# A fused attention and expert kernel: the sums made beside batch 1, X's mixed inputs, and the second layer's first blocks

## The chip, the cores and the metric

The kernel runs on 1 core of one Trainium2 chip. The metric is the time of one execution on the device in microseconds (us), lower is better. The five engines of the core run their own instruction lists: TensorE (PE, with its weight loads shown apart as PEld), VectorE (DVE), ScalarE (ACT), GpSimd (POOL) and SyncE (SP, which here issues nearly all DMAs).

## The reference

```python
def reference(**kwargs):
    ...
    attn_out = _attn_ref(**attn_kwargs)          # 2 x 8 heads x 576 x 64, threshold before the softmax
    x = np.ascontiguousarray(attn_out.transpose(0, 2, 1, 3)).reshape(B * S, H * D)   # 1152 x 512
    x = _moe_ref(x=x, **moe_kwargs)
    return _moe2_ref(x=x, **moe2_kwargs)

def _moe_ref(x, w1, w2, w3, w_out):
    h = np.maximum(np.maximum(x @ w1, x @ w2), x @ w3)    # 512 -> 768
    return (h @ w_out).astype(np.float32)                 # 768 -> 512

def _moe2_ref(x, domain_probs, w1, w2):
    p = domain_probs / (domain_probs.sum(-1, keepdims=True) + 1e-09)
    for e in range(4):
        h = np.maximum(x @ w1[e], 0.0)                    # 512 -> 1024
        out += p[:, e:e + 1] * (h @ w2[e])                # 1024 -> 512
    return out
```

## The kernel before

Every product is made in float32 precision from two parts of each operand: a high half (a copy by ACT, called hi) and a low half (operand less high half, called lo, mostly by POOL), and three matmuls per product. The 1152 rows are worked in two groups: group 0 holds 512 rows of batch 0, group 1 the other 640, batch 1 and the 64 left over.

The order in time is: attention of batch 0; then the first layer (`layer_max`) and the four experts (`experts`) of group 0, and beside the experts the attention of batch 1 (`attention_slow`); then group 1's first layer and experts, which save products by Strassen's scheme (`mixed_pair`: seven products in place of eight, on sums and differences of quarter blocks).

**What sets the order.** All matmuls of the layers form one stream (`Stream`), which counts the columns that it has passed through TensorE. Loads, halves and sums of weights are hooks with a column at which they are written into the program (`plan.at(use - lag, fn)`: so many columns ahead of their use). The results of a product are taken out of PSUM 1000, 2000, ... columns after it. `attention_slow` is a generator: at each yield the main program lets the stream go on by `PACE` columns (L1213 to L1217). PE, DVE, ACT and POOL then run in the order written. SP's order is left to the scheduler. So an instruction that waits holds up all that stands behind it on its engine.

**One step of `attention_slow`** has four yields: scores (`qk`, L331) and their maximum; exponential on ACT (`power`, L349); threshold and row sum on DVE (`weigh`, L354); normalization on POOL (`norm`, L362). The weights of the step before are transposed on PE (`turn`, L372) in the second quarter. A job has 9 steps; four jobs make batch 1. The next job's K and Q are prepared beside it (`prep`, L176 on): transposed, halved (KN on ACT L187 and DVE L189), the 64 remaining rows of k transposed into another PSUM buffer (L192), and spread over the partitions by ten DMAs from SP (L203, L205, L206 and L219).

**Sums for group 1.** A pair of weight blocks needs four sums of its quarters (`quarter_sums`, L845). They are made beside batch 1, by POOL, half a pair at a time (`sums_ahead`): a load, the sums 8000 columns later, a store to DRAM 11000 columns later, one such set every `AHEAD` = 14500 columns, 22 sets. `pair_block` then loads them (tile s) with the raw block (wraw), and makes the halves dh, dl, sh, sl with the lags of LAGS_X or LAGS_PAIR.

**X's mixed inputs** (`mixed_x`, L824): eight differences of quarters of X by DVE (`less`, L809), each with a high half by ACT (L814) and a low half by DVE (L817). They are made after batch 1's attention, in front of group 1's first product, one step for each 1024 columns.

**Blocks of w_out** for group 1 (`weights64` with g = 1, names o0_0 to o3_1): loaded 20000, high half 8000 and low half 6500 columns ahead of use (LAGS_KEPT).

Raw weight blocks use a ring of four buffers (`raw`); their high and low halves are tiles a (first matrix) and b (second matrix).

Of the kernel before, what the change touches and what calls it, by code (L numbers as in the profile page):

```python
# [22 lines left out]
def fused_kernel(ctx: ExitStack, tc: tile.TileContext, q, k, v, tau, w1, w2, w3, w_out, probs, m_w1, m_w2, out):  # L23
    nc = tc.nc
# [24 lines left out]
    LAGS_FIRST = (("words", 60000), ("exponent", 50000), ("low3", 49000), ("clamp", 48000), ("merge", 47000), ("sign", 46000), ("keep", 45000), ("hi", 10500), ("lo", 9000))  # L49
    LAGS_KEPT = (("load", 20000), ("hi", 8000), ("lo", 6500))  # L50

    LAGS_A = ((1.05, 1, 1.4, 1.9), (3, 3, 3, 1.9))
# [13 lines left out]
    START = 13000  # L66
    PACE = 2000
    STACKED = 10000
# [107 lines left out]
    def prep(job):  # L176
# [12 lines left out]
        nc.vector.tensor_tensor(out=KN[:, 1, 0:MAIN], in0=tk, in1=f32(KN[:, 0, 0:MAIN]), op=ALU.subtract)  # L189
        yield  # L190
        tr = ptile_at("U", [P, REM + P])
        nc.tensor.transpose(tr[:, 0:REM], flat(kr), ident[0:REM, 0:REM])  # L192
# [533 lines left out]
    def weights64(g, name, use, src, shape):  # L726
        kept["planned"] = kept.get("planned", 0) + 1
        return block(use, shape, "a", NA, None, (LAGS_FIRST if kept["planned"] <= EARLY else LAGS64, LAGS_KEPT)[g], name, g, src if g == 0 else None)

# [94 lines left out]
    def mixed_x():  # L824
        steps = []
        for c in range(KC // 2):
            b11, b12, b21, b22 = (part("x", d, cols) for d in (c, KC // 2 + c) for cols in (left, right))
            steps += [less(b11, b12, b11), *cut("x", 0, c, b11), less(b12, b22, b12), less(b22, b22, b11),
                      *cut("x", 1, c, b22), *cut("x", 2, c, b12), less(b21, b21, b22), *cut("x", 3, c, b21)]
        return steps  # L830

# [9 lines left out]

    def quarter_sums(S, A):

        for out, a, b, op in ((0, A(1, 0), A(1, 1), ALU.add), (1, S(0), A(0, 0), ALU.subtract), (2, A(0, 0), A(1, 0), ALU.subtract), (3, A(0, 1), S(1), ALU.subtract)):
            nc.gpsimd.tensor_tensor(out=S(out), in0=a, in1=b, op=op)  # L845

    def sums_ahead(when, key, half):
        b = {}

        def load():  # L850
            b["raw"] = atile([P, 2, 2, P], F32, "sraw")
            for i in range(2):
                nc.sync.dma_start(out=b["raw"][:, i], in_=half(i))

        def sums():
            b["s"] = atile([P, 4, P], F32, "ssum")
            quarter_sums(lambda x: b["s"][:, x, :], lambda i, j: b["raw"][:, i, j, :])

        def store():
            key, c = b["key"]  # L860
            if ("s", key) not in kept:
                kept["s", key] = dp.tile([P, 4, 2, P], F32, name=f"kept_s{key}")
            nc.sync.dma_start(out=kept["s", key][:, :, c, :], in_=b["s"])

        b["key"] = key
        for fn, lag in ((load, 0), (sums, 8000), (store, 11000)):
            plan.at(when + lag, fn)

    def pair_block(use, src, lags, key=None):
# [3 lines left out]
        def load():  # L873
            b["raw"] = mix_tile([P, KC, 2 * P], F32, "wraw")
            if isinstance(src, tuple):
                nc.sync.dma_start(out=b["raw"][:, :, 0:P], in_=kept[src[0]])
                nc.sync.dma_start(out=b["raw"][:, KC // 2:KC, P:2 * P], in_=kept[src[1]][:, KC // 2:KC, :])
            else:
                nc.sync.dma_start(out=b["raw"], in_=src)
# [4 lines left out]
        def sums():  # L884
            if key is None:
                quarter_sums(lambda x: b["s"][:, x, :, :], raw)

# [73 lines left out]

    LAGS_X = (27000, 26000, 12800, 11800, 10800, 11600, 9500, 6800)
    LAGS_PAIR = (
        (44000, 30000, 27500, 26500, 25500, 26000, 23500, 21000),
        (44000, 29000, 26500, 25500, 24500, 23500, 21000, 18500))
    LAGS_SOON = ((44000, 42000, 40000, 39000, 37000, 38000, 34000, 30000), (44000, 42000, 36000, 34000, 32000, 33000, 28000, 23000))
    AHEAD = 14500

    def max_mixed():
# [31 lines left out]
        for f in range(0, NF, 2):  # L1001
            for w in range(3):
                for c in range(2):
                    sums_ahead(MAX0 + 10000 + AHEAD * k, (f"w{w}_{f}", c), lambda i, w=w, f=f, c=c: kept[f"w{w}_{f + i}"][:, c::2, :])
                    k += 1
                b = pair_block(plan.cols, (f"w{w}_{f}", f"w{w}_{f + 1}"), LAGS_X, f"w{w}_{f}")
                mixed_pair(b, "x", X[1], finish(f, w), (1, 5, 6, 7, 2, 4, 3))
        for f in range(0, NF2 // 2, 2):
            for c in range(2):
                rows = m_w1[0].rearrange("(j c p) f -> c p j f", j=2, p=P)[c]  # L1010
                sums_ahead(MAX0 + 10000 + AHEAD * k, (f"e{f}", c), lambda i, f=f, rows=rows: rows[:, :, (f + i) * P:(f + i + 1) * P])
                k += 1
# [139 lines left out]
    bufs_a = {"K12": 2, "QS": 2, "V": 2, "VR": 2, "em": 3, "am": 6, "ar": 4}  # L1152
    bufs_b = {"K12": 2, "QS": 2, "em": 2, "am": 4, "ar": 2}
    for bf in (bufs_a, bufs_b):
# [67 lines left out]
    while steps or mo["waiting"]:  # L1222
        if steps:
            steps.popleft()(None)
        if mo["waiting"]:
            mo["waiting"].pop(0)()
        goal = stream.now + 1024
        while stream.now < min(goal, END0):
# [43 lines left out]
```

## Time and profile before

| | |
|---|---|
| median of 3 runs | 730.0 us (729.4 to 730.63) |
| the profiled execution: its own time | 727.51 us |
| its span | 725.7 us, 11937 instructions |
| PE busy | 689.6 us (95%), 3897 matmuls |
| DVE, ACT, POOL busy | 471.2, 355.9, 498.9 us |
| DMA | 97.01 MB, mean 134 GB/s |

The span runs from the first to the last instruction of the program in the profile; the execution's own time has 1.8 us around it. Busy time is time in which an engine executes. An engine that is often idle costs nothing by that; what counts is where TensorE, the busiest, has holes and what ended each.

### The profile page before, as it was taken

What the parts mean: (1) busy time and instruction counts of PE and PEld (TensorE: products, weight loads), DVE (VectorE), ACT (ScalarE), POOL (GpSimd) and SP (SyncE); (2) the same over time, 40 slices, a digit from 0 to 9 for tenths busy, and PEclk for the clock granted to TensorE, in tenths of its full rate; (3) what the DMA queues carried; (4) which work ended last, traced back from release to release, by engine and by line L of the source; (5) the groups of instructions that cost most, each with busy time, mean ns of one, the idle gap of its engine ahead of it and who ended that gap; (6) DMA issues with size and microseconds to landing.
All of it is one profiled execution on the core that took longest, in us unless ns stands there. A gap on an engine that the chain in (4) does not pass through costs nothing.

```text
span 725.7 us, 11937 instructions
## 1 busy us (share of the span) xinstructions
PE 689.6 (95%) x3897; PEld 608.0 (84%) x3897; DVE 471.2 (65%) x1116; ACT 355.9 (49%) x760; POOL 498.9 (69%) x590
## 2 busy tenths in 40 slices
PE   5988899999989999999999989999999999999997
PEld 4877789777868888878878869999988998998995
DVE  6898897776357776767676556773835644644652
ACT  5777775545345455454545343436434434433430
POOL 4778885777585776586686465868587679669650
PEclk9899999999999999999999999999999999999999
DMA  6644605877878648567343544453322222222103
GB/s 188 156 102 103 184 1 170 267 226 220 226 214 203 169 115 223 142 157 186 103 142 106 184 126 149 148 159 91 106 84 67 88 88 75 78 81 88 60 1 72
DMA packets 116482, 97.01 MB, mean 134 GB/s; under 512 B 27332, under 2 KB 97988, under 8 KB 116420
## 3 DMA queue, kind: packets, MB, share of 16 engines
q1 hardware_dynamic: 115970, 95.96, 47.2%
q8 instruction: 31, 0.51, 0.3%
q10 hardware_dynamic: 418, 0.30, 0.2%
q14 instruction: 31, 0.25, 0.1%
q0 software_dynamic: 32, 0.00, 0.0%
HBM read 69.88 MB, written 14.42 MB: 116 GB/s over the span
## 4 chain that ended last, share of the span: by engine, by line
PE 71%; POOL 8%; DVE 7%; issue 6%; ACT 4%; DMA 3%; SPq 1%; POOLq 0%; DVEq 0%; ACTq 0%
PE ps L1120 59%; PE u L449 4%; PE s L331 3%; PE t L372 2%; POOL a L673 2%; DVE em L354 2%; DMA words<-in_moe_w_dram 1%; DVE st_negm L342 1%; POOL b L673 1%; POOL ssum L845 1%; POOL em L362 1%; ACT em L349 1%; POOL b L702 1%; DMA krem<-in_k_dram 1%; DVE raw L710 1%
## 5 line engine op out<-in xcount | busy, mean ns | idle before, releaser
L1120 PE MATMUL ps<-b,hh 128*128 128x512 f32 x576 | 185.3, 395 | 1.6 <-ACT hh L1070 1.2
L1120 PEld LDWEIGHTS ps<-b,hh 128*128 128x128 f32 x576 | 108.1, 189 | 23.8 <-issue 1.6
L673 POOL TENSOR_TENSOR b<-raw,b 128x512 fp32r<-128x512 f32 x64 | 82.9, 1301 | 64.5 <-ACT b L669 64.4
L1120 PE MATMUL ps<-b,hl 128*128 128x512 f32 x288 | 114.1, 396 | 0.4 <-DVE hl L1073 0.4
L673 POOL TENSOR_TENSOR a<-raw,a 128x512 fp32r<-128x512 f32 (+1 forms) x66 | 80.6, 1223 | 45.2 <-ACT a L669 37.4
L1089 DVE SCALAR_TENSOR_TENSOR acc<-ps,pr,acc 128x512 f32<-128x512 f32 x63 | 47.2, 749 | 77.5 <-PE ps L1120 77.5
L362 POOL TENSOR_SCALAR em<-em,st_r,even 128x576 f32<-128x576 f32 x70 | 57.6, 824 | 42.8 <-DVE st_r L361 39.4
L349 ACT ACTIVATE em<-s,st_negm 128x576 f32<-128x576 f32 x72 | 53.3, 742 | 63.3 <-DVE st_negm L342 57.0
L1120 PE MATMUL ps<-y0h,a 128*128 128x512 f32 x256 | 83.4, 397 | 0.0
L342 DVE TENSOR_REDUCE st_negm<-s 128x1 f32<-128x576 f32 x72 | 54.1, 753 | 41.2 <-PE s L331 41.0
L1120 PE MATMUL ps<-bt,sh 128*128 128x320 f32 x300 | 70.1, 309 | 0.0
L354 DVE SCALAR_TENSOR_TENSOR em<-s,st_thr,em 128x576 f32<-128x576 f32 x72 | 58.4, 812 | 9.5 <-ACT em L349 7.2
L669 ACT ACTIVATE a<-raw 128x512 fp32r<-128x512 f32 (+1 forms) x66 | 39.7, 604 | 50.2 <-DVE raw L710 17.7
L915 POOL TENSOR_TENSOR sl<-s,sh 128x512 fp32r<-128x512 f32 x50 | 64.1, 1303 | 0.0
L1120 PEld LDWEIGHTS ps<-b,hl 128*128 128x128 f32 x288 | 54.6, 189 | 10.9 <-DVE hl L1073 0.8
L902 POOL TENSOR_TENSOR dl<-wraw,dh 128x512 fp32r<-128x512 f32 (+1 forms) x50 | 49.9, 1018 | 13.9 <-ACT dh L897 13.9
L331 PE MATMUL s<-K,QS 128*128 128x288 f32 x264 | 49.9, 313 | 7.9 <-DVE em L354 7.0
L1020 ACT ACTIVATE hh<-ps 128x320 fp32r<-128x320 f32 x64 | 27.4, 439 | 54.1 <-DVE ps L948 54.1
L1120 PEld LDWEIGHTS ps<-y0h,a 128*128 128x128 f32 x256 | 47.0, 189 | 7.9
L331 PEld LDWEIGHTS s<-K,QS 128*128 128x128 f32 x264 | 41.7, 197 | 13.5 <-issue 5.2
L1120 PE MATMUL ps<-y0l,a 128*128 128x512 f32 x128 | 51.4, 402 | 0.0
L1120 PEld LDWEIGHTS ps<-bt,sh 128*128 128x128 f32 x300 | 51.2, 188 | 0.0
(205 smaller groups left out, 1704.7 us busy)
## 6 DMA issues: line engine op xcount, KB each, us to landing
raw<-in_moe_w_dram SPq DMA_DIRECT2D x96, 256.0 KB, 3.1
words<-in_moe_w_dram SPq DMA_DIRECT2D x18, 512.0 KB, 5.7
wraw<-in_moe_w_dram SPq DMA_DIRECT2D x16, 512.0 KB, 3.4
kept_w<-raw SPq DMA_DIRECT2D x18, 256.0 KB, 2.4
sraw<-kept_w SPq DMA_DIRECT2D x36, 128.0 KB, 2.6
kept_sw<-ssum SPq DMA_DIRECT2D x18, 256.0 KB, 3.2
s<-kept_sw SPq DMA_DIRECT2D x9, 512.0 KB, 4.5
K<-KN SPq DMA_DIRECT2D x14, 288.0 KB, 5.3
```

Source lines behind the costliest of these rows:

```text
L331: nc.tensor.matmul(st.s[:, kh, 0:HS], lhsT=l, rhs=r, start=i == 0, stop=i == len(terms) - 1)
L342: nc.vector.tensor_reduce(out=st.stat["negm"], in_=views(st)[0], op=ALU.max, axis=AX.XY, negate=True)
L349: return nc.scalar.activation(out=ev, in_=sv, func=AF.Exp, bias=st.stat["negm"])
L354: nc.vector.scalar_tensor_tensor(out=ev, in0=sv, scalar=st.stat["thr"], in1=ev, op0=ALU.is_ge, op1=ALU.mult, accum_out=st.stat["sum"])
L362: last = (nc.vector if swift else nc.gpsimd).tensor_scalar(out=em, in0=em, scalar1=re, scalar2=even, op0=ALU.mult, op1=ALU.add)
L449: at["valued"] = nc.tensor.matmul(pv, lhsT=l, rhs=r, start=i == 0, stop=i == len(terms) - 1)
L669: nc.scalar.activation(out=b["hi"], in_=b["raw"], func=AF.Copy)
L673: nc.gpsimd.tensor_tensor(out=b["lo"], in0=b["raw"], in1=f32(b["hi"]), op=ALU.subtract)
L902: nc.gpsimd.tensor_tensor(out=rows(b["dl"], x), in0=src, in1=f32(rows(b["dh"], x)), op=ALU.subtract)
L915: nc.gpsimd.tensor_tensor(out=rows(b["sl"], slice(x, x + 2)), in0=rows(b["s"], slice(x, x + 2)), in1=f32(rows(b["sh"], slice(x, x + 2))), ...
L1089: nc.vector.scalar_tensor_tensor(out=accs[t], in0=ps, scalar=pe, in1=accs[t], op0=ALU.mult, op1=ALU.add)
L1120: nc.tensor.matmul(ps, lhsT=l, rhs=r, start=i == 0, stop=i == count - 1)
```

## The change

It does these things:

- `sums_ahead`: the sums come 14000 columns behind their load (8000 before) and the store 17000 (11000); the set is summed into a tile of the ring `hmax` of three buffers (before, one buffer `ssum`); the raw halves get two buffers (`sraw`). A set begins every 17500 columns (14500), the first 4000 columns earlier.
- The first matrix's pairs other than the first (w0_2 and w0_4) have no sums made ahead: their blocks are loaded whole, and DVE makes the sums behind the load. 18 sets are left of 22.
- `PACE` is 2100 (2000), and `prep` of batch 1 has one more yield, ahead of the transposes of k's remainder.
- `mixed_x`: all differences first, then all high halves, then all low halves; two steps for each 768 columns.
- Blocks o0_0, o0_1 and o1_0: load, high and low half 30000, 16000 and 14500 columns ahead of use.
- LAGS_X: halves of the pairs mostly 400 to 1200 columns earlier.

```diff
+    LAGS_KEPT_FIRST = (("load", 30000), ("hi", 16000), ("lo", 14500))
...
-    PACE = 2000
+    PACE = 2100
...
         nc.vector.tensor_tensor(out=KN[:, 1, 0:MAIN], in0=tk, in1=f32(KN[:, 0, 0:MAIN]), op=ALU.subtract)
         yield
+        if job.b:
+            yield
         tr = ptile_at("U", [P, REM + P])
...
-        return block(use, shape, "a", NA, None, (LAGS_FIRST if kept["planned"] <= EARLY else LAGS64, LAGS_KEPT)[g], name, g, src if g == 0 else None)
+        return block(use, shape, "a", NA, None, (LAGS_FIRST if kept["planned"] <= EARLY else LAGS64, LAGS_KEPT_FIRST if name in ("o0_0", "o0_1", "o1_0") else LAGS_KEPT)[g], name, g, src if g == 0 else None)
...
     def mixed_x():
-        steps = []
+        subs, cuts = [], []
         for c in range(KC // 2):
             b11, b12, b21, b22 = (part("x", d, cols) for d in (c, KC // 2 + c) for cols in (left, right))
-            steps += [less(b11, b12, b11), *cut("x", 0, c, b11), less(b12, b22, b12), less(b22, b22, b11),
-                      *cut("x", 1, c, b22), *cut("x", 2, c, b12), less(b21, b21, b22), *cut("x", 3, c, b21)]
-        return steps
+            subs += [less(b11, b12, b11), less(b12, b22, b12), less(b22, b22, b11), less(b21, b21, b22)]
+            cuts += [cut("x", x, c, src) for x, src in enumerate((b11, b22, b12, b21))]
+        return subs + [fn for step in zip(*cuts) for fn in step]
...
-            b["s"] = atile([P, 4, P], F32, "ssum")
+            b["s"] = wtile([P, 4, P], F32, "hmax", 3)
...
-        for fn, lag in ((load, 0), (sums, 8000), (store, 11000)):
+        for fn, lag in ((load, 0), (sums, 14000), (store, 17000)):
             plan.at(when + lag, fn)
...
-                nc.sync.dma_start(out=b["raw"][:, KC // 2:KC, P:2 * P], in_=kept[src[1]][:, KC // 2:KC, :])
+                half = slice(0 if key is None else KC // 2, KC)
+                nc.sync.dma_start(out=b["raw"][:, half, P:2 * P], in_=kept[src[1]][:, half, :])
...
-                quarter_sums(lambda x: b["s"][:, x, :, :], raw)
+                quarter_sums(lambda x: b["s"][:, x, :, :], raw, nc.vector if isinstance(src, tuple) else nc.gpsimd)
...
-    LAGS_X = (27000, 26000, 12800, 11800, 10800, 11600, 9500, 6800)
+    LAGS_X = (27000, 18000, 14000, 12500, 11200, 12600, 10000, 7200)
...
-    AHEAD = 14500
+    AHEAD = 17500
...
-                for c in range(2):
-                    sums_ahead(MAX0 + 10000 + AHEAD * k, (f"w{w}_{f}", c), lambda i, w=w, f=f, c=c: kept[f"w{w}_{f + i}"][:, c::2, :])
+                ahead = f == 0 or w > 0
+                for c in range(2 if ahead else 0):
+                    sums_ahead(MAX0 + 6000 + AHEAD * k, (f"w{w}_{f}", c), lambda i, w=w, f=f, c=c: kept[f"w{w}_{f + i}"][:, c::2, :])
...
-    bufs_b = {"K12": 2, "QS": 2, "em": 2, "am": 4, "ar": 2}
+    bufs_b = {"sraw": 2, "K12": 2, "QS": 2, "em": 2, "am": 4, "ar": 2}
...
-        if steps:
+        for _ in range(min(2, len(steps))):
             steps.popleft()(None)
         if mo["waiting"]:
             mo["waiting"].pop(0)()
-        goal = stream.now + 1024
+        goal = stream.now + 768
```

Three places show how it moves instructions. The number of matmuls stays.

SP, where batch 1's first job is prepared; raw is a weight block, K12 and QS the spread K and Q, sraw a half set for the sums. Before:

```order
L205 DMA K12_2699<-KN_2701 64x2x64 x2
L219 DMA QS_2700<-knat_2786 64x512
L219 DMA QS_2700<-qnat_2787 64x512
L219 DMA QS_2700<-knat_2786 64x512
L219 DMA QS_2700<-qnat_2787 64x512
L863 DMA kept_sw0_0_2816<-ssum_2791 512x1x128
L677 DMA raw_2818<-in_moe2_w1_dram 128x4x128
L853 DMA sraw_2836<-kept_w0_0_201 128x2x128
L853 DMA sraw_2836<-kept_w0_1_1886 128x2x128
L677 DMA raw_2850<-in_moe2_w1_dram 128x4x128
```

And now:

```order
L856 DMA sraw_2822<-kept_w0_0_201 128x2x128
L856 DMA sraw_2822<-kept_w0_1_1886 128x2x128
L209 DMA K12_2699<-KN_2701 64x2x512
L680 DMA raw_2749<-in_moe2_w2_dram 128x512
L209 DMA K12_2699<-KN_2701 64x2x512
L680 DMA raw_2811<-in_moe2_w1_dram 128x4x128
L152 DMA diagonal_76<-in_q_dram 64x64
L680 DMA raw_2850<-in_moe2_w1_dram 128x4x128
L206 DMA K12_2699<-KN_2701 64x2x576 x2
L208 DMA K12_2699<-KN_2701 64x2x64 x2
L222 DMA QS_2700<-knat_2798 64x512
L866 DMA kept_sw0_0_2819<-hmax_2801 512x1x128
```

The second half set and the next two blocks of the first expert matrix stand ahead of most of the ten transfers, and no longer behind them.

POOL, from one normalization to the next, in the second job's third step (V is that job's value block, a a low half of a weight block). Before:

```order
L273 TENSOR_TENSOR V_3724<-vnat_2938,V_3724 128x8x64
L279 TENSOR_TENSOR VR_3725<-vnrem_2940,VR_3725 64x64 x2
L673 TENSOR_TENSOR a_3776<-raw_3681,a_3747 128x512
L845 TENSOR_TENSOR ssum_3801<-sraw_3732 128x128
L845 TENSOR_TENSOR ssum_3801<-ssum_3801,sraw_3732 128x128
L845 TENSOR_TENSOR ssum_3801<-sraw_3732 128x128
L845 TENSOR_TENSOR ssum_3801<-sraw_3732,ssum_3801 128x128
L362 TENSOR_SCALAR em_3756<-em_3756,st_r_3760,even_113 128x576
```

And now:

```order
L276 TENSOR_TENSOR V_3743<-vnat_2952,V_3743 128x8x64
L676 TENSOR_TENSOR a_3765<-raw_3683,a_3758 128x512
L282 TENSOR_TENSOR VR_3744<-vnrem_2954,VR_3744 64x64 x2
L848 TENSOR_TENSOR hmax_3821<-sraw_3701 128x128
L848 TENSOR_TENSOR hmax_3821<-hmax_3821,sraw_3701 128x128
L848 TENSOR_TENSOR hmax_3821<-sraw_3701 128x128
L848 TENSOR_TENSOR hmax_3821<-sraw_3701,hmax_3821 128x128
L676 TENSOR_TENSOR a_3826<-raw_3736,a_3814 128x512
L365 TENSOR_SCALAR em_3773<-em_3773,st_r_3777,even_113 128x576
```

A second low half has come into this gap. In the fourth job's third step the four sums have left the gap, and V, its remainders and one low half remain.

ACT, ahead of the last hidden block (hh) of group 0; bt is a mixed input, b a high half of a weight block. Before:

```order
L814 ACTIVATE bt_5667<-whole_2828 128x320
L1070 ACTIVATE hh_5673<-ps_5628 128x512
L814 ACTIVATE bt_5687<-whole_2832 128x320
L669 ACTIVATE b_5690<-raw_5641 128x512
L814 ACTIVATE bt_5700<-whole_2828 128x320
L1070 ACTIVATE hh_5704<-ps_5665 128x512
L669 ACTIVATE b_5713<-raw_5662 128x512
L814 ACTIVATE bt_5717<-whole_2832 128x320
L1070 ACTIVATE hh_5736<-ps_5698 128x512
L897 ACTIVATE dh_5769<-wraw_5725 128x512
```

And now:

```order
L1075 ACTIVATE hh_5636<-ps_5594 128x512
L672 ACTIVATE b_5647<-raw_5591 128x512
L817 ACTIVATE bt_5651<-whole_2839 128x320
L817 ACTIVATE bt_5654<-whole_2843 128x320
L817 ACTIVATE bt_5661<-whole_2839 128x320
L817 ACTIVATE bt_5664<-whole_2843 128x320
L817 ACTIVATE bt_5674<-whole_2841 128x320
L817 ACTIVATE bt_5677<-whole_2845 128x320
L817 ACTIVATE bt_5683<-whole_2841 128x320
L817 ACTIVATE bt_5686<-whole_2845 128x320
L1075 ACTIVATE hh_5690<-ps_5631 128x512
L901 ACTIVATE dh_5724<-wraw_5667 128x512
```

The eight high halves stand in a row, where before each stood between other work.

## Rows read from the trace of the kernel before

**Rows 1.** Windows by stage: busy us of each engine (instructions), granted clock, DMA share, GB/s.
```profile
185.00:214.00 29.00, 26.62 (x122) 21.29 (x121) 14.39 (x33) 13.15 (x28) 21.32 (x32) 0.94 0.86 226
214.00:410.00 196.00, 192.92 (x1057) 164.25 (x1056) 134.37 (x335) 100.25 (x208) 131.79 (x179) 1.00 0.57 152
410.00:430.00 20.00, 17.93 (x76) 13.84 (x75) 13.03 (x22) 10.95 (x23) 10.79 (x9) 1.00 0.45 149
430.00:490.00 60.00, 60.00 (x399) 59.10 (x398) 40.10 (x90) 20.97 (x48) 41.72 (x39) 1.00 0.52 161
490.00:526.00 36.00, 34.84 (x235) 34.25 (x234) 22.10 (x47) 20.67 (x49) 25.67 (x25) 1.00 0.32 96
```

**Rows 2.** Timeline of PE: start us, us, instruction, count, [idle before, and what ended it].
```profile
201.88 0.77 PE L331 MATMUL s<-K,QS 128*128 128x288 f32 x4 [0.28 <-issue]
...
205.55 0.68 PE L372 MATMUL t<-ident,em 128*128 128x128 f32 x4 [1.98 <-POOL em L362]
...
319.40 0.27 PE L192 MATMUL u<-ident,knrem 64*128 64x64 f32 x1 [1.39 <-DVE st_sum L360]
...
372.45 0.66 PE L372 MATMUL t<-ident,em 128*128 128x128 f32 x4 [1.40 <-POOL em L362]
...
402.42 0.62 PE L1120 MATMUL ps<-b,hh 128*128 128x512 f32 x2
402.88 0.39 PE L1120 MATMUL ps<-b,hl 128*128 128x512 f32 x1
...
425.47 0.47 PE L1120 MATMUL ps<-b,hh 128*128 128x512 f32 x1 [1.22 <-ACT hh L1070]
...
502.61 0.55 PE L1120 MATMUL ps<-hh,a 128*128 128x320 f32 x2 [1.16 <-POOL a L673]
```

**Rows 3.** Windows: the stretch behind the hole at 205.55; the granted clock stands third from the end.
```profile
206.00:209.50 3.50, 3.50 (x11) 2.82 (x10) 1.11 (x4) 2.11 (x7) 3.35 (x6) 0.51 0.82 220
```

**Rows 4.** Timelines of SP and ACT, 195 to 200 us.
```profile
195.03 0.59 SPq L219 DMA_DIRECT2D QS<-qnat  x1
...
196.35 0.65 SPq L677 DMA_DIRECT2D raw<-in_moe_w_dram  x1
...
199.66 0.63 ACT L669 ACTIVATE a<-raw 128x512 fp32r<-128x512 f32 x1 [5.97 <-DMA raw<-in_moe_w_dram]
```

**Rows 5.** DMA issues of the raw halves for sums: count, KB each, median us to landing.
```profile
sraw<-kept_w SPq DMA_DIRECT2D x36, 128.0 KB, 2.6
```

**Rows 6.** Timelines of ACT and DVE ahead of the hole at 319.40.
```profile
316.69 0.60 ACT L1070 ACTIVATE hh<-ps 128x512 fp32r<-128x512 f32 x1
...
317.32 0.69 DVE L1073 SCALAR_TENSOR_TENSOR hl<-ps,hh 128x512 fp32r<-128x512 f32 x1 [2.05 <-ACT hh L1070]
```

**Rows 7.** Instructions of L362, 200 to 400 us: count, ns min/median/max, first and last start.
```profile
L362 POOL TENSOR_SCALAR em<-em,st_r,even x36: 816/823/830, 204.7 to 396.5; 128x576 f32<-128x576 f32 x36
```

**Rows 8.** Timeline of POOL: two pairs of successive normalizations.
```profile
264.84 0.82 POOL L362 TENSOR_SCALAR em<-em,st_r,even 128x576 f32<-128x576 f32 x1 [0.31 <-DVE st_r L361]
...
270.74 0.82 POOL L362 TENSOR_SCALAR em<-em,st_r,even 128x576 f32<-128x576 f32 x1
...
364.49 0.82 POOL L362 TENSOR_SCALAR em<-em,st_r,even 128x576 f32<-128x576 f32 x1
...
371.58 0.82 POOL L362 TENSOR_SCALAR em<-em,st_r,even 128x576 f32<-128x576 f32 x1
```

**Rows 9.** Costliest groups: low halves of weight blocks on POOL; busy us, mean ns of one.
```profile
L673 POOL TENSOR_TENSOR b<-raw,b 128x512 fp32r<-128x512 f32 x64 | 82.9, 1301 | 64.5 <-ACT b L669 64.4
```

**Rows 10.** Timelines of DVE and ACT, 411 to 425 us.
```profile
411.52 1.01 DVE L809 TENSOR_TENSOR whole<-whole 128x320 f32<-128x320 f32 x2
...
412.56 0.83 ACT L814 ACTIVATE bt<-whole 128x320 fp32r<-128x320 f32 x2 [2.68 <-DVE whole L809]
...
424.37 0.47 ACT L814 ACTIVATE bt<-whole 128x320 fp32r<-128x320 f32 x1 [1.86 <-DVE whole L809]
```

**Rows 11.** Timelines of ACT and POOL ahead of the hole at 502.61.
```profile
494.66 0.53 ACT L669 ACTIVATE a<-raw 128x384 fp32r<-128x384 f32 x1 [0.79 <-PE ps L1120]
...
501.57 1.97 POOL L673 TENSOR_TENSOR a<-raw,a 128x384 fp32r<-128x384 f32 x2
```

More of the change, by code (lines that the diff above doesn't have):

```diff
@@ L840, in mixed_y, with quarter_sums @@
         return [less(t2, None, t2), *cut("y", 3, c, t2), hi, lo]
-    def quarter_sums(S, A):
+    def quarter_sums(S, A, eng=nc.gpsimd):
         for out, a, b, op in ((0, A(1, 0), A(1, 1), ALU.add), (1, S(0), A(0, 0), ALU.subtract), (2, A(0, 0), A(1, 0), ALU.subtract), (3, A(0, 1), S(1), ALU.subtract)):
-            nc.gpsimd.tensor_tensor(out=S(out), in0=a, in1=b, op=op)
+            eng.tensor_tensor(out=S(out), in0=a, in1=b, op=op)
     def sums_ahead(when, key, half):
@@ L1002, in max_mixed @@
             for w in range(3):
-                for c in range(2):
-                    sums_ahead(MAX0 + 10000 + AHEAD * k, (f"w{w}_{f}", c), lambda i, w=w, f=f, c=c: kept[f"w{w}_{f + i}"][:, c::2, :])
+                ahead = f == 0 or w > 0
+                for c in range(2 if ahead else 0):
+                    sums_ahead(MAX0 + 6000 + AHEAD * k, (f"w{w}_{f}", c), lambda i, w=w, f=f, c=c: kept[f"w{w}_{f + i}"][:, c::2, :])
                     k += 1
-                b = pair_block(plan.cols, (f"w{w}_{f}", f"w{w}_{f + 1}"), LAGS_X, f"w{w}_{f}")
+                b = pair_block(plan.cols, (f"w{w}_{f}", f"w{w}_{f + 1}"), LAGS_X, f"w{w}_{f}" if ahead else None)
                 mixed_pair(b, "x", X[1], finish(f, w), (1, 5, 6, 7, 2, 4, 3))
@@ L1010, in max_mixed @@
                 rows = m_w1[0].rearrange("(j c p) f -> c p j f", j=2, p=P)[c]
-                sums_ahead(MAX0 + 10000 + AHEAD * k, (f"e{f}", c), lambda i, f=f, rows=rows: rows[:, :, (f + i) * P:(f + i + 1) * P])
+                sums_ahead(MAX0 + 6000 + AHEAD * k, (f"e{f}", c), lambda i, f=f, rows=rows: rows[:, :, (f + i) * P:(f + i + 1) * P])
                 k += 1
```

## The prediction

> **What bounds the kernel now.** I read the busy time by stage first, then the TensorE timeline for its holes, and for each hole the timelines of the engine that ended it.
>
> TensorE (PE) is the bound. In [rows 1] it is busy for 192.92 of the 196 us of the stretch that holds most of batch 1's attention. While it runs, a 512-column matmul starts every 0.23 us: two start between 402.42 and 402.88 [rows 2]. Neither kernel changes the number of matmuls, so the change can give back only holes. Behind 185 us, where the two programs part, [rows 1] leaves these: 2.38 us idle up to 214, 3.08 us up to 410, 2.07 us up to 430 and 1.16 us between 490 and 526. The modelled end of a matmul hides some 0.15 us of each hole: the one at 205.55 is 1.98 us by its idle time, and 2.13 us by the starts.
>
> The large holes are in [rows 2]. I call them **A** (205.55, waits for POOL's normalization), **B** (319.40, waits for DVE), **C** (372.45, POOL again), **D** (four holes up to 426.2, the largest at 425.47) and **E** (502.61, waits for POOL's low half of a w_out block).
>
> A has a second price. Behind it TensorE's granted clock is 0.51 for 3.5 us [rows 3], that is the lower of its two levels, 1.2 instead of 2.4 GHz, and that work takes twice as long: 0.49 x 3.5 = 1.7 us. Behind B, C, D and E the stretches of [rows 1] show 1.00.
>
> **The change part by part, on the profiled execution** (727.5 us, span 725.7; the median of the runs shown is 730.0, 2.5 us more, and I carry that over).
>
> *Earlier, fewer sums; their order on SP.* In A the normalization was late because ACT stood still for 5.97 us, to 199.66, for a raw weight block [rows 4]: the exponential stands behind it on ACT, and the block's low half ahead of the normalization on POOL. The block's load had been issued only at 196.35, behind the ten transfers that spread K and Q, the last at 195.03, and a store of sums. In the new order two raw blocks (raw_2811, raw_2850) stand ahead of most of these transfers. Each issue takes SP about 0.65 us, and the first of the spreading transfers waits for the same DVE result, so these two start near 189 and 190 and are there near 193, before ACT asks for them. The third stands behind the transfers and is needed only after the first exponential. What pays is the last Q transfer: four issues later, 2.6 us, near 197.6, against scores that come 1.4 us later (ten passes 100 columns longer and one pass of 2100 more: 3100 columns) and whose second group, the first to read Q, started at 201.88 [rows 2]. With a landing of 2.6 us, as half a block of sums takes [rows 5], some 3 us cover it. So A goes: 2.38 us idle, 0.3 us hidden, 1.7 us of clock, of which I leave 0.3: **4.1 us**.
>
> The lag itself matters less: 8000 columns are 16 matmuls, 3.6 us, against the 2.6 us of [rows 5]. The Trainium skill ("DMA: Bandwidth & Descriptors", section "Anatomy of one DMA — SWDGE (gpsimd) path") gives 2.0 us plus the bytes over 436 GB/s for one DMA of another queue kind, 2.3 us for these 128 KB, and by it a lag of 8000 is long enough, so that the longer lag buys nothing and A hangs on SP's order alone; the trace's 2.6 us agrees in size.
>
> *One pass more before the transposes of k's remainder.* B: ACT reached hh at 316.69 behind K's copy and a weight block, DVE waited 2.05 us for it [rows 6] and so came late to K's low half, whose PSUM buffer the transposes at 319.40 need. One pass is 2100 columns, 0.93 us, plus the attention's own matmuls in it; with that the hole shrinks from 1.39 + 0.15 to nothing: **1.5 us**. That PE would otherwise have met the next late normalization is part of the new collisions below.
>
> *Pass of 2100, sums every 17500.* POOL normalizes once in 191.8/35 = 5.48 us [rows 7]. What it does between two normalizations decides. In C that took 371.58 - 364.49 = 7.09 us, with the same parts (V, two V remainders, a low half, four sums) as the 5.90 us from 264.84 to 270.74, which cost nothing [rows 8]. Now the sums have left C's place (the order shows it), so C goes: **1.55 us**. But in the second job they stay, and a second low half of 1.30 us [rows 9] joins them: 7.2 us. Lower bound: 7.2 less the free 5.9 less four passes of 100 columns (0.18 us) = 1.1; upper bound: C's own 1.56. I take **1.1 us lost**. In the other 35 gaps I count at most 6.2 us, which the old order had too.
>
> *X's mixed inputs by kind, two steps in each 768 columns.* In D ACT and DVE took turns: difference, high half, low half of one input, ACT waiting 1.86 us at 424.37 [rows 10], and the copy hh behind it ended the hole at 425.47. Now eight differences come first (0.50 us each), then eight high halves on ACT (0.83 us for two) and eight low halves on DVE. Counted from the end of the third block's matmuls, ACT has that block's hh at 0.7 and a weight block at 1.2, the eight high halves end near 4.5, the last hh at 5.0. PE asks for it after 12 + 9 matmuls, 4.8 us. DVE's hl behind it (ahead of it there stand eight differences, from -1.4 on, one hl and two low halves, to 4.2) ends near 5.6, asked for at 5.1. I leave 0.5 us of 2.07 + 4 x 0.15: **2.2 us**. The price, if the last attention block comes late: each high half that is not done then delays hh by some 0.4 us.
>
> *Second layer's first blocks.* E waits for block o2_0, and only o0_0, o0_1 and o1_0 come sooner. POOL is busy without a pause from o1_1's low half on, whose high half waits for PE at 494.66, to the low half of o2_0 at 501.57 [rows 11]; that row of work is the same in the new order. E stays: nothing. The three blocks hide it no further, and the earlier loads only move SP's waits.
>
> *Two pairs' sums on DVE* (eight operations, by the 0.50 us for 320 columns under 4 us in all) and the fuller loads lie between 430 and 490, where PE has no hole at all [rows 1]: nothing; without that cover, 4 us at most. The lags of LAGS_X likewise.
>
> *New collisions.* The old 36 steps had two holes of some 1.5 us from in-order engines (B and C). With 5% more room for a step, I take half of one: **0.7 us lost**; bounds 0 and two, 3.1.
>
> Sum: 4.1 + 1.5 + 1.55 + 2.2 - 1.1 - 0.7 = 7.55 us. Span 718.1, this execution 719.9, median **722.4 us**.
>
> **The rivals.**
>
> 1. *The order on SP still holds up the raw blocks.* Then the longer lag gives nothing, and ACT stands before a raw block again: the third is still behind SP's row of transfers. For it: SP's row has grown by four issues. Against: two blocks have passed it. A stays: 7.55 - 4.1 = 3.45, 726.5 us. The rule of the Trainium skill above ("DMA: Bandwidth & Descriptors", the same section) is on this rival's side as to the lag.
>
> 2. *Slower: the sums sit in a bad place for several sets in succession.* A step is now 8400 columns and a set comes every 17500, so that a set moves by 700 columns against the normalization; before, it moved by 1500 of 8000. Eight of the 18 sets then begin within 3500 columns ahead of a normalization, and four sums of 0.46 us last 4100 columns. If each costs what C did, 8 x 1.55 = 12.4 against 4.1 + 1.5 + 2.2 = 7.8 won: 734.6 us. It turns slower than before from the sixth on. For it: the 7.2 us gap; against: only three gaps hold over 5.5 us.
>
> 3. *No change: other collisions take the place of B and C.* Every pass shifts against the stream, and six new holes of 1.5 us, in 36 steps that had two, eat 9 us of the 8.25 won without the 0.7: 730.7 us. For it: any in-order engine that waits for PE can make one; against: POOL has four sets less and steps are longer.
>
> **How the numbers follow.** Forecast 0.74, rival 1 0.12, rival 2 0.07, rival 3 0.07. A measurement tells 0.2% (1.5 us) from no change. Faster is the forecast and rival 1: 0.86; same is rival 3: 0.07; slower rival 2: 0.07. Low end: A, B, C, D wholly gone, E too, nothing new, 4.4 + 1.5 + 1.55 + 2.7 + 1.3 = 11.5 us, 718.5; with the small holes between, 718.2. High end: rival 1's 726.5 with a little of another collision, 727.0.
>
> **What would show it.** Right: no wait of several us on ACT for a raw block near 200 us, clock 1.00 there, PE 410 to 430 within 0.5 us of full, a hole of about 1 us in the second job's third step, and E unchanged at 1.2 us. Wrong: a hole over 2 us anywhere behind 200 us (it may bring the lower clock back), POOL late by over 1.5 us at several successive normalizations, or a changed busy time before 185 us.

## The result, and the profile after

The changed kernel takes **722.18 us** (median of four runs, 721.87 to 723.39), the kernel before 729.79 us on the same chip: a ratio of **0.9897**, 95% interval 0.988 to 0.9914. The profiled execution took 722.14 us (span 720.2), 5.4 us less than that of before, whose own profile was 2.3 us faster than its median.

Of this difference in the profiles, part lies where the two programs are the same. The same hole ahead of the parting, a wait for GpSimd's hl, stands 0.57 us later in the profile after. The first fence is the TensorE timeline before, the second the same view after (a line is start, busy us, engine, line, operation, and in brackets the idle time ahead and what ended it):

```profile
167.48 0.50 PE L1120 MATMUL ps<-hl,a 128*128 128x512 f32 x1 [1.59 <-POOL hl L764]
```

```profile
168.05 0.50 PE L1125 MATMUL ps<-hl,a 128*128 128x512 f32 x1 [1.56 <-POOL hl L767]
...
368.27 0.66 PE L375 MATMUL t<-ident,em 128*128 128x128 f32 x4 [0.22 <-POOL em L365]
...
416.79 0.50 PE L1125 MATMUL ps<-b,hl 128*128 128x512 f32 x1 [0.19 <-DVE hl L1078]
...
418.98 0.47 PE L1125 MATMUL ps<-b,hh 128*128 128x512 f32 x1 [1.46 <-ACT hh L1075]
...
427.63 0.50 PE L1125 MATMUL ps<-b,hh 128*128 128x512 f32 x1 [0.96 <-DVE acc L1094]
...
497.17 0.56 PE L1125 MATMUL ps<-hh,a 128*128 128x320 f32 x2 [1.16 <-POOL a L676]
```

From that hole to the end the profile after is (725.7 - 167.48) - (720.2 - 168.05) = 6.1 us shorter. I call this the gain behind 168 and give it for the experiments too, since the start of the program differs between executions: this hole stands between 167.23 and 170.79 us in them, and all edits act behind it.

The large holes of [rows 2] answer like this: A, B and C are gone. D has three holes instead of four and is half a us larger. E is there to the hundredth: 1.16 us. By stage, answering to [rows 1] (busy us of each engine in the stretch, TensorE first, then the granted clock, DMA share and GB/s):

```profile
185.00:214.00 29.00, 28.78 (x140) 23.57 (x139) 15.64 (x36) 14.95 (x32) 23.00 (x34) 1.00 0.88 235
214.00:410.00 196.00, 195.46 (x1067) 166.94 (x1066) 134.15 (x333) 100.00 (x207) 126.22 (x163) 1.00 0.54 142
410.00:430.00 20.00, 17.39 (x76) 13.55 (x75) 18.10 (x22) 10.00 (x23) 14.08 (x11) 1.00 0.53 168
430.00:490.00 60.00, 60.00 (x408) 59.63 (x407) 45.04 (x102) 24.23 (x56) 39.78 (x39) 1.00 0.46 142
490.00:526.00 36.00, 34.84 (x223) 33.54 (x223) 21.50 (x44) 20.19 (x48) 27.79 (x27) 1.00 0.34 99
```

The first stretch has 0.22 us idle instead of 2.38, and the clock is 1.00 instead of 0.94 (0.06 x 29 = 1.7 us): 3.9 us won. The second has 0.54 instead of 3.08: 2.5 us won. The third has 2.61 instead of 2.07: **0.5 us lost, where the prediction had 2.2 won**. The last is the same. Together 5.9 us, which is the 6.1 of above within what the edges of stretches move.

What removed A is to be seen on SP. Its timeline after, answering to [rows 4]:

```profile
185.69 1.18 SPq L856 DMA_DIRECT2D sraw<-kept_w  x2
187.97 0.63 SPq L209 DMA_DIRECT2D K<-KN  x1
188.71 0.54 SPq L680 DMA_DIRECT2D raw<-in_moe_w_dram  x1
...
190.12 0.55 SPq L680 DMA_DIRECT2D raw<-in_moe_w_dram  x1
...
191.87 0.54 SPq L680 DMA_DIRECT2D raw<-in_moe_w_dram  x1
...
199.56 0.59 SPq L222 DMA_DIRECT2D QS<-qnat  x1
```

Of the ten transfers that spread K and Q, the last eight now stand behind three raw blocks, and all ten behind both halves of a set of raw columns for the sums (sraw, 185.69). Before, only the block at 187.46 was so far ahead; the next block and the set were issued behind the last transfer, at 196.35 [rows 4] and 197.04:

```profile
187.46 0.53 SPq L677 DMA_DIRECT2D raw<-in_moe_w_dram  x1
...
197.04 1.22 SPq L853 DMA_DIRECT2D sraw<-kept_w  x2
```

Now the first exponential on ScalarE and its normalization on GpSimd wait for the attention alone (st_negm is the row maximum, st_r the reciprocal sum). ScalarE:

```profile
196.16 0.63 ACT L672 ACTIVATE a<-raw 128x512 fp32r<-128x512 f32 x1 [0.86 <-DMA raw<-in_moe_w_dram]
201.24 0.74 ACT L352 ACTIVATE em<-s,st_negm 128x576 f32<-128x576 f32 x1 [4.45 <-DVE st_negm L345]
```

GpSimd:

```profile
198.85 1.29 POOL L676 TENSOR_TENSOR a<-raw,a 128x512 fp32r<-128x512 f32 x1
203.42 0.82 POOL L365 TENSOR_SCALAR em<-em,st_r,even 128x576 f32<-128x576 f32 x1 [3.28 <-DVE st_r L364]
```

In D, VectorE carries X's steps in batches. Its timeline after (L812 a difference, L820 a low half, hl the low half of an expert's activations, for which TensorE waits):

```profile
410.85 5.28 DVE L812 TENSOR_TENSOR whole<-whole 128x320 f32<-128x320 f32 x6
416.05 0.68 DVE L1078 SCALAR_TENSOR_TENSOR hl<-ps,hh 128x512 fp32r<-128x512 f32 x1
...
418.87 0.69 DVE L1078 SCALAR_TENSOR_TENSOR hl<-ps,hh 128x512 fp32r<-128x512 f32 x1 [0.31 <-ACT hh L1075]
419.48 7.44 DVE L820 TENSOR_TENSOR bt<-whole,bt 128x320 fp32r<-128x320 f32 x6
426.84 2.06 DVE L1094 SCALAR_TENSOR_TENSOR acc<-ps,pr,acc 128x512 f32<-128x512 f32 x3
```

Six differences took 5.28 us, 0.88 each, and six low halves 7.44, or 1.24 each, where the prediction counted 0.50. The hl at 416.05 waited behind six differences (hole at 416.79); the copy hh on ScalarE stood behind three high halves that waited for the last differences (hole at 418.98, ScalarE's row below); and acc, which empties a PSUM bank, behind six low halves (hole at 427.63).

```profile
412.33 0.60 ACT L1075 ACTIVATE hh<-ps 128x512 fp32r<-128x512 f32 x1 [1.29 <-PE ps L1125]
...
417.17 1.19 ACT L817 ACTIVATE bt<-whole 128x320 fp32r<-128x320 f32 x3 [1.05 <-DVE whole L812]
418.26 0.57 ACT L1075 ACTIVATE hh<-ps 128x512 fp32r<-128x512 f32 x1
```

### The profile page after: what moved, and what is told of

Same layout as the page of the kernel before. It is cut to its first block, busy times and chain, and to the rows that moved or that the text cites. A ratio compares the mean times of both kernels' runs of the same rounds, so it can differ in the third digit from the quotient of the medians.

```text
span 720.2 us, 11890 instructions
## 1 busy us (share of the span) xinstructions
PE 687.9 (96%) x3897; PEld 607.8 (84%) x3897; DVE 479.2 (67%) x1124; ACT 355.7 (49%) x760; POOL 493.5 (69%) x574
## 4 chain that ended last, share of the span: by engine, by line
PE 72%; DVE 10%; POOL 6%; issue 4%; ACT 4%; DMA 3%; SPq 1%; DVEq 0%; POOLq 0%; ACTq 0%
PE ps L1125 59%; PE u L452 4%; PE s L334 4%; PE t L375 3%; POOL a L676 2%; DVE em L357 2%; DMA words<-in_moe_w_dram 1%; DVE st_negm L345 1%; DVE bt L820 1%; ACT em L352 1%; DVE raw L713 1%; POOL b L705 1%; DVE whole L812 1%; DMA krem<-in_k_dram 1%; DMA raw<-in_moe_w_dram 1%
```

## Experiments

Three questions: which part removed A, what became of the 2.2 us in D, and what E hangs on. Times are medians with the ratio to the kernel before on the same chip (its median there was 728.9 to 729.4 us); "behind 168" is the gain of the profiled execution as above (after: 6.1).

### 1. Only the extra pass

The kernel before, with two lines of the change:

```diff
+        if job.b:
+            yield
         tr = ptile_at("U", [P, REM + P])
```

> The kernel before with one thing of the change: the extra pass ahead of the transposes of k's remainder. Theory (the raw block's place on SP decides hole A): the pass moves two raw blocks ahead of the K and Q transfers by itself, so A (2.1 us idle by the starts and 1.7 us of clock, 4.1 in the prediction's sum) goes, and B's 1.5 us with it, while C, D and E stay: 729.8 - 5.6 = 724.2 us, no hole over 1 us near 200 and the clock at 1.00 there. Rival (the sums' longer lag and lower number remove A): only B goes, A stays with its lower clock: 728.3 us.

Measured: 730.39 us, ratio 1.0022 (1.0005 to 1.004): slower, behind 168 a loss of 2.6 us. Neither theory: A did not go, it became two holes. TensorE:

```profile
206.51 0.66 PE L374 MATMUL t<-ident,em 128*128 128x128 f32 x4 [2.00 <-POOL em L364]
212.98 0.66 PE L374 MATMUL t<-ident,em 128*128 128x128 f32 x4 [1.75 <-POOL em L364]
```

ScalarE's wait of several us for a raw block ahead of the first exponential was gone (0.78 us was the longest there). But GpSimd stood still instead, for the columns that the sums need:

```profile
202.58 0.46 POOL L847 TENSOR_TENSOR ssum<-sraw 128x128 f32<-128x128 f32 x1 [6.04 <-DMA sraw<-kept_w]
```

That set was issued at 198.88, behind the last Q transfer. So two loads had to pass the transfers. B was gone, as expected. D grew (3.47 us idle from 410 to 430, 2.07 before, and a granted clock of 0.94 there), which made it slower than before.

### 2. Only the sums

The kernel before with lags 14000 and 17000, `AHEAD` 17500, the first set 4000 columns sooner, two raw buffers, two pairs' sums on VectorE.

> The kernel before with the part on the sums alone (lags 14000 and 17000, interval 17500, start 6000, two raw buffers, two pairs' sums on VectorE). Theory (place on SP): the block that ScalarE waits for still stands behind the last Q transfer, one issue sooner than before since the store of sums is gone there, so A loses 0.6 us of its wait at most and its clock stays low; C may go, because the sums leave its place: 729.8 - 0.6 - 1.5 = 727.7 us, 729.2 if C stays. Rival (lag and number of the sums remove A): A goes, 729.8 - 4.1 - 1.5 = 724.2 us.

Measured: 726.23 us, 0.996 (0.9942 to 0.9978), behind 168 3.4 us won. A stayed (1.66 us idle at 208.02), and now it was ScalarE that stood ahead of the first exponential for a raw block:

```profile
202.11 0.63 ACT L669 ACTIVATE a<-raw 128x512 fp32r<-128x512 f32 x1 [5.10 <-DMA raw<-in_moe_w_dram]
```

C was gone; a hole of 1.24 us (by the starts) at 397.81 was new. The clock stayed at 1.00 behind this A, which the expected 727.7 us had not counted on: that is 1.7 us.

### 3. The sums and the extra pass together

Both edits of 1 and 2; pass of 2000 columns, X's steps in the old order.

> The kernel before with the sums' part and the extra pass together, pass length 2000 and X's steps in the old order. Theory (two loads had to pass the K and Q transfers, the raw block that ScalarE waits for and the raw columns that GpSimd's sums wait for; the pass alone moved the one, the sums alone the other): no hole over 0.5 us between 190 and 215, clock 1.00 there, B gone; the stretch 200 to 400 loses 7 us of idle time against before (13.2 to some 6, as in the changed kernel at 2000 columns), X's steps cost what they cost before or up to 3 us more: 729 - 7.2 + (0 to 3) = 722 to 725 us. Rival (A went through the longer pass or something else of the change): a hole of over 1.5 us stays near 205, 727 us or more.

Measured: 725.0 us, 0.9939 (0.9916 to 0.9963). No hole from 190 to 215, clock 1.00, and the exponential and the normalization wait for the attention alone. From 200 to 400 us TensorE is busy for 199.15 us, 194.54 before, at a clock of 1.00 instead of 0.99. **With a pass of 2000 columns, A needs both parts**: the sums alone leave the raw block behind the transfers, the pass alone leaves the sums' columns there. What this kernel loses again lies in D (3.34 us idle from 410 to 430 and a granted clock of 0.91); the largest hole:

```profile
421.30 0.77 PE L1124 MATMUL ps<-b,hh 128*128 128x512 f32 x1 [2.22 <-ACT hh L1074]
```

### 4. Without the extra pass

The changed kernel less the two lines of 1.

> The changed kernel without the extra pass. The raw block then stands behind the six K transfers and ahead of the four of Q. Theory (place on SP): issued some 3 us sooner than before (four issues of 0.65 us and a store of sums), so ScalarE's wait of 5.97 us shrinks to about 3 and A is gone or under 0.5 us, but B's 1.4 us hole is back: 722.2 + 1.5 = 723.7 us, up to 724.2. Rival (only a place ahead of K's transfers helps): A is back with its clock, 722.2 + 1.5 + 4.1 = 727.8 us. A third (B does not come back, since the steps are longer): 722.2 us.

Measured: 728.9 us, 0.9998 (0.9982 to 1.0014). A stayed away, with the raw block behind K's six transfers but ahead of Q's four (TensorE busy 28.98 of 29 us from 185 to 214): so it is enough to pass the last four transfers, and with the rest of the change, the longer pass among it, the extra pass isn't needed for A. Which part stands in for it no run shows. B's kind came back, in an earlier job (217.84, 1.06 us by the starts). The rest of the loss no theory had: D idles 4.32 us, and the clock from 410 to 430 is 0.86 (2.8 us). One pass moves all later steps against the stream; that D grows by this phase is argued, not shown apart.

### 5. The sums' load 6000 columns later

```diff
-        for fn, lag in ((load, 0), (sums, 14000), (store, 17000)):
+        for fn, lag in ((load, 0), (sums, 8000), (store, 11000)):
...
-                    sums_ahead(MAX0 + 6000 + AHEAD * k,
+                    sums_ahead(MAX0 + 12000 + AHEAD * k,
```

> The changed kernel with the sums' loads 6000 columns later and the sums and stores where they are (lags 8000 and 11000): GpSimd's order is the same, and the load still stands ahead of the K and Q transfers. Theory (the place on SP decides, not the lag): 722.2 us, within 0.7, no hole near 205. Rival (8000 columns are too short a lag once SP has a row to issue): GpSimd waits for sraw at several sets, 1 to 2 us each at two or more of them, 724 us or more.

Measured: 722.9 us, 0.9907 (0.9885 to 0.9929), behind 168 6.4 us: no difference to the change. But the edit moved little: SP issued 17 of the 18 sets within 1.5 us of their places in the changed kernel (counted from the hole at 168, which stands 0.8 us sooner here). Both sets near A are still ahead of the transfers. Only the third set moved, by 4.7 us (issued at 201.42 in the changed kernel), and GpSimd waited for it. SP and GpSimd:

```profile
182.61 3.00 SPq L856 DMA_DIRECT2D sraw<-kept_w  x4
205.30 1.18 SPq L856 DMA_DIRECT2D sraw<-kept_w  x2
```

```profile
209.80 0.46 POOL L848 TENSOR_TENSOR hmax<-sraw 128x128 f32<-128x128 f32 x1 [0.43 <-DMA sraw<-kept_w]
```

So A stays away with the lags of the kernel before, and with the second set written 5000 columns later than there (12000 + 17500 against 10000 + 14500). What a shorter time between load and sums would cost stays open. By the estimate that the prediction weighed (the Trainium skill, "DMA: Bandwidth & Descriptors", section "Anatomy of one DMA — SWDGE (gpsimd) path") such a load is there after 2.3 us. The trace does not agree: from issue to landing it took 3.9 us at the median here, more than the 3.6 us of 8000 columns (count, KB each, median us):

```profile
sraw<-kept_w SPq DMA_DIRECT2D x28, 128.0 KB, 3.9
```

### 6. X's steps in the old order

The changed kernel with `mixed_x` and its pace (one step in 1024 columns) as before.

> The changed kernel with the steps of X's mixed inputs in the old order, one in 1024 columns. Theory (the new order did gain what was predicted, but the later end of attention gave it back): the old order here is worse than in the kernel before, since its 24 steps took 17 us there and now start 6 us later against TensorE; D grows from 3.1 to 5 us or more: 722.2 + 2.2 = 724.4 us, more if a hole brings the lower clock. Rival (the order of the steps is worth nothing): 722.2 us.

Measured: **720.81 us**, 0.9876 (0.9855 to 0.9897), behind 168 8.6 us. The theory fell. The rival can't be excluded by time alone, since the interval overlaps that of the change (0.988 to 0.9914); the profile speaks against it, for D has 0.29 us idle instead of 2.61:

```profile
410.00:430.00 20.00, 19.71 (x90) 16.01 (x89) 15.25 (x24) 11.14 (x24) 10.04 (x9) 1.00 0.54 177
```

So between the two profiles the new order of X's steps cost about 2.5 us, where it was to win 2.2. D had gone through the phase: the longer passes end batch 1's attention 36 x 4 x 100 = 14400 columns later against the stream (28 matmuls of 512 columns, 6.4 us), so that two of the hl are out of the way when the steps begin, and two and four operations stand ahead of the other two.

### 7. Pass of 2000

```diff
-    PACE = 2100
+    PACE = 2000
```

> The changed kernel with a pass of 2000 columns. Theory (the longer pass only gives GpSimd room between two normalizations, and costs the steps of X's mixed inputs their lead: 36 steps of 4 passes of 100 columns are 6.4 us): the steps come 6.4 us sooner against TensorE, D falls from 3.1 to under 1 us, and in exchange the second job's third step and others make holes of about 1.5 us each in GpSimd's rows: two of them, 722.2 - 2.1 + 3.0 = 723.1 us. Rival (the pass length sets neither): 722.2 us. Other rival (the longer pass is what removed A): a hole of over 1.5 us near 205, 726 us.

Measured: 725.72 us, 0.9949 (0.9931 to 0.9968). The sign was right, the place wrong: no late normalization worth the name, but one hole of 4.46 us in D. VectorE:

```profile
411.23 8.18 DVE L820 TENSOR_TENSOR bt<-whole,bt 128x320 fp32r<-128x320 f32 x8
419.33 1.87 DVE L1078 SCALAR_TENSOR_TENSOR hl<-ps,hh 128x512 fp32r<-128x512 f32 x3
```

All eight low halves stand ahead of three hl, and TensorE waits for the first of these. With 3 and 6 this makes a square (idle time of TensorE and its granted clock from 410 to 430):

| with the sums and the extra pass | X's steps in the old order | by kind |
|---|---|---|
| pass of 2000 | 725.0 us; 3.34 idle, 0.91 | 725.72 us; 4.46, 0.91 |
| pass of 2100 | 720.81 us; 0.29, 1.00 | 722.18 us; 2.61, 1.00 |

(The upper left has LAGS_X and the lags of o0_0 to o1_0 as before, too.) D idles more by kind in both rows, and less with the longer pass in both columns. By time the longer pass is faster in both columns; between the two orders the intervals overlap in both rows.

### 8. The new order of X's steps alone

The kernel before with the new `mixed_x`, two steps in 768 columns.

> The kernel before with the new order of X's mixed inputs alone (kind by kind, two steps in 768 columns). Theory (kind by kind puts six low halves ahead of three hl on VectorE): D grows from 2.9 us to 4.5 or more and brings the lower clock, 729.0 + 1.7 + 1.0 = 731.7 us. Rival (the prediction's term, 2.2 us gained): 726.8 us. Rival (nothing either way): 729.0 us.

Measured: 728.49 us, 0.9985 (0.9969 to 1.0001). It can't be told from no change. The loss of the theory (a ratio of 1.004) lies outside the interval; the 2.2 us of the prediction (0.997) lie at its very edge and are not excluded. So that the order by kind costs something is seen at the phase of the changed kernel alone. There is no profile of it that can be compared, so what D is here stays open.

### 9. Four differences sooner

The changed kernel; X's first four differences need only heads that are done, and go into the last passes of the attention:

```diff
-    for x in attention_slow(rest, cycle(MODES_B)):
+    steps = deque(mixed_x())
+    for n, x in enumerate(attention_slow(rest, cycle(MODES_B))):
+        if 161 <= n < 165:
+            steps.popleft()(None)
```

> The changed kernel with the first four differences of X's mixed inputs made during the last four passes of the attention, where VectorE stands idle for several us. Theory (hole D stayed, because eight differences, slowed from 0.5 to 0.9 us by GpSimd's work beside them, stand ahead of hl and of the high halves): D shrinks from 3.1 us to 1 or less: 722.2 - 2.1 = 720.1 us. Rival (D hangs on ScalarE's own row and on the order of the first mixed product, not on the differences): no change, 722.2 us. If a difference now delays the last block of attention instead: 723 us.

Measured: 723.42 us, 0.9923 (0.9901 to 0.9945), behind 168 3.8 us. A miss that shows the mechanism. TensorE has one hole of 2.93 us at 420.83, behind which the clock is 0.50 for 5 us. VectorE:

```profile
402.49 0.83 DVE L812 TENSOR_TENSOR whole<-whole 128x320 f32<-128x320 f32 x1
...
404.28 1.00 DVE L812 TENSOR_TENSOR whole<-whole 128x320 f32<-128x320 f32 x2
...
414.98 5.21 DVE L820 TENSOR_TENSOR bt<-whole,bt 128x320 fp32r<-128x320 f32 x6
420.10 0.68 DVE L1078 SCALAR_TENSOR_TENSOR hl<-ps,hh 128x512 fp32r<-128x512 f32 x1
```

The differences did move into idle time. But six low halves still stand ahead of the last hl. The first two rows show the price of GpSimd beside it: the difference at 402.49 took 0.83 us while GpSimd made a low half (401.67 to 402.97), the two at 404.28 took 0.50 each while it was idle.

### 10. Four differences sooner, low halves spaced

9, with all halves in order of use and one low half in 1536 columns:

```diff
+        cuts = cuts[0::4] + cuts[1::4] + cuts[2::4] + cuts[3::4]
...
-        for _ in range(min(2, len(steps))):
+        for _ in range(min(2 if len(steps) > KC * 2 else 1, len(steps))):
...
-        goal = stream.now + 768
+        goal = stream.now + (768 if len(steps) > KC * 2 else 1536)
```

> The changed kernel with four differences made during the last four passes of attention, and behind them one low half in each 1536 columns, so that only two of them stand ahead of the last hl on VectorE (six did in the run with the four early differences alone). Theory (D is VectorE's in-order row: its operations take 0.9 us beside GpSimd's instead of 0.5, and too many of them stand ahead of an hl): no hole over 0.5 us between 410 and 430, 722.2 - 2.6 = 719.6 us. Rival (the holes there come from ScalarE's row or from the order of the first mixed product): over 1.5 us are left, 722 us or more.

Measured: **718.78 us**, 0.985 (0.9828 to 0.9872), behind 168 9.8 us. D is gone, although the low halves still take 1.0 to 1.3 us each:

```profile
410.00:430.00 20.00, 20.00 (x96) 16.67 (x95) 16.82 (x20) 10.08 (x23) 14.71 (x12) 1.00 0.63 199
```

Only two of them stand ahead of the last hl. (The order among the halves changed with the spacing; the two were not run apart.) This is the theory's case: what counts is not how much VectorE has to do, but what is written ahead of the result that TensorE waits for.

### 11. Block o2_0's low half on VectorE

```diff
-            nc.gpsimd.tensor_tensor(out=b["lo"], ...
+            (nc.vector if g == 1 and name == "o2_0" else nc.gpsimd).tensor_tensor(out=b["lo"], ...
```

> The changed kernel with the low half of block o2_0 on VectorE instead of GpSimd. Theory (E is GpSimd's row of work ahead of that low half): the low half follows its high half (ends near 495.0) by 1 us and hole E, 1.32 us, goes: 722.2 - 1.2 = 721.0 us. Rival (E hangs on the high half's buffer or on the load): E stays, 722.2 us.

Measured: 721.77 us, 0.9894 (0.9875 to 0.9914). By time alone no difference to the change; behind 168 7.5 us, 1.4 more than the change, and E is 0.18 us idle:

```profile
498.13 0.57 PE L1126 MATMUL ps<-hh,a 128*128 128x320 f32 x2 [0.18 <-POOL a L676]
```

So E was GpSimd's row of work ahead of that low half, as the prediction had it.

### 12. The best version

10 with the low halves of o2_0 and o2_1 on VectorE.

> The run with the spaced low halves of X and, besides, the low halves of blocks o2_0 and o2_1 on VectorE. Theory: E's 1.32 us goes, and with the second block also the 0.34 us that were left when only o2_0 moved: 718.8 - 1.3 = 717.5 us. Rival (the two changes disturb each other, a hole elsewhere takes the place of E): 718.8 us.

Measured: **717.19 us**, 0.9839 (0.9813 to 0.9864), behind 168 10.5 us. It beats both kernels; against 10 the intervals overlap, and a later block's low half on GpSimd leaves 0.4 us of E (490 to 526: 35.56 of 36 us busy).

## Why the prediction was right, and where it was not

The forecast 722.4 us stands beside 722.18. That it is so close is luck: against the profile the sum was 7.55 us, and 6.1 came; the median moved by 7.6 since the profile of before was a fast one. And two errors in the sum took each other back in part: from 214 to 410 us 1.3 us more came than forecast, in D 2.7 less.

**A (4.1 forecast, 3.9 measured): right in size and place, half right in cause.** SP's order decides, as the prediction said. But it named one load, the raw block, and put the term under the sums. Runs 1 to 3 show two loads behind the transfers, each enough to hold up the normalization, and that the extra pass moved the raw block, while the part on the sums moved their own. Each part alone leaves a hole of over 1.6 us. Within the part on the sums it is neither the longer lag nor the earlier start, by 5; left is the second raw buffer, since with one buffer a load waits for the sums of the set before; that is argued, no run has it alone. The prediction looked at what ended the last wait in front of the hole; GpSimd's own wait in the kernel before, of 5.75 us, was put down in the trace to a load of the sums' columns, and I passed over it:

```profile
200.38 1.29 POOL L673 TENSOR_TENSOR a<-raw,a 128x512 fp32r<-128x512 f32 x1 [5.75 <-DMA sraw<-kept_w]
```

(That low half also needs ScalarE's high half, which ended near 200.3: the two waits ended together.) The last Q transfer came at 199.56, 2 us later than forecast, and was in time. So was the second of the two raw blocks: issued at 191.87, it kept ScalarE waiting for 0.86 us, to 196.16, where the prediction had it there near 193.

**B (1.5) and C (1.55): right.** Both holes are gone from their places. One pass brings B or takes it (1, 4), and the sums leave C (2).

**The second job's third step (1.1 lost): the gap right, the price not.** GpSimd needed 7.1 us between two normalizations, and 7.2 were counted:

```profile
263.78 0.82 POOL L365 TENSOR_SCALAR em<-em,st_r,even 128x576 f32<-128x576 f32 x1 [0.62 <-DVE st_r L364]
...
270.91 0.81 POOL L365 TENSOR_SCALAR em<-em,st_r,even 128x576 f32<-128x576 f32 x1
```

No hole follows that the timeline lists. With the **new collisions (0.7 lost)**, 1.8 us were charged; the whole stretch from 214 to 410 has 0.54 us idle.

**D (2.2 won): the step that failed.** It was lost by 0.5. The order on VectorE came as the prediction has it: ahead of the last hl stand eight differences, one hl and two low halves. The start did, too: the third block's hh ends at 412.93, which the prediction calls 0.7, and the first difference starts at 410.85, which is -1.4. What failed is the price, "eight differences come first (0.50 us each)". The first six took 0.88 each, and the later six low halves 1.24, because GpSimd worked beside them; the last two differences, with GpSimd idle (1.08 us for both at 416.65), kept the price. GpSimd:

```profile
411.29 1.54 POOL L676 TENSOR_TENSOR b<-raw,b 128x512 fp32r<-128x512 f32 x1
413.53 1.33 POOL L676 TENSOR_TENSOR b<-raw,b 128x512 fp32r<-128x512 f32 x1 [0.70 <-ACT b L672]
```

So the last hh ended at 418.83, or 6.6 where the prediction had 5.0, and TensorE waited 1.46 us for it. For the six low halves behind the last hl, which hold up acc (0.96 us), the sum had no term. The trace of before had dear rows, and I took the cheap ones. VectorE, and GpSimd beside it:

```profile
421.54 1.32 DVE L817 TENSOR_TENSOR bt<-whole,bt 128x320 fp32r<-128x320 f32 x1 [0.39 <-ACT bt L814]
```

```profile
421.23 2.76 POOL L673 TENSOR_TENSOR b<-raw,b 128x512 fp32r<-128x512 f32 x2 [2.98 <-ACT b L669]
```

The Trainium skill says so, too ("SBUF — State Buffer", section "SBUF: two separate sides"): VectorE operations with two SBUF inputs and GpSimd exclude each other from a shared port pair. The trace agrees: hl, which reads one input from PSUM, takes 0.68 us beside GpSimd's work (420.10 in run 9) and 0.68 without it (416.05 after).

The prediction also credited the gain to the order. By 3, 6 and 7 it comes with the longer pass (through the phase, I argue), and the order by kind takes most of it back.

**E (nothing): right**, 1.16 us before and after, and 11 shows its cause.

The rivals: 1 was wrong that A stays; that the longer lag buys nothing fits run 5, which moved one set alone. 2 and 3 did not come: no late normalization idles TensorE by over 0.22 us.

## What to carry to other kernels

On in-order engines the unit of cost is what is written ahead of the instruction that the bound engine waits for. Spread steps so that one or two stand ahead of each such result; grouping them by kind makes rows of six or eight. Price a step by rows in which the neighbouring engine works as it will in the new order. A change in pace is a change in phase for everything behind it: follow it to the next stage before pricing another part there. And when a hole has a wait behind it, look for a second one: two engines waited here for two loads in the same row on SP, and with either one alone removed the hole was still there.

## What the runs showed of the hardware

The granted clock does not follow from the hole alone. Between 37 and 42 us all these kernels run the same instructions with the same two holes (0.8 and 1.2 us idle). Behind them the clock was 1.00 in the changed kernel (first fence, stretch from 40 to 46, columns as above) and 0.72 in run 9 (second fence), as in runs 7 and 12:

```profile
40.00:46.00 6.00, 4.53 (x34) 4.33 (x35) 5.68 (x21) 4.65 (x12) 4.58 (x6) 1.00 0.03 8
```

```profile
40.00:46.00 6.00, 5.27 (x29) 5.07 (x30) 4.59 (x15) 3.60 (x10) 4.33 (x6) 0.72 0.01 2
```

Likewise a hole of 2.00 us at 206.51 in run 1 left the clock at 1.00, and the 1.98 us of A in the kernel before took it to 0.51. So the 1.7 us of clock in A's term may hold for the one profiled execution alone; what other executions paid there is not known.
